# A gated attention and mixer kernel on one core: the order of the last four output parts, and of the first K chunk's pieces

## The chip, the core and the metric

The kernel runs on one core of a Trainium2 chip. The core has five engines that run side by side and meet at semaphores: TensorE (PE, with its weight loads shown apart as PEld), VectorE (DVE), ScalarE (ACT), GpSimd (POOL) and SyncE (SP), which only issues DMAs here. ACT issues a few DMAs as well. Products land in PSUM, which PE writes and DVE and ACT read; the rest lies in SBUF. The metric is the device time of one execution in microseconds, as the median of several runs.

## The reference, cut to what matters

Two blocks work on the same x (2048 rows, 640 columns), and a gate per row mixes their outputs.

```python
g = sigmoid((x * gate_w).sum(-1, keepdims=True))
# A: linear attention, 32 heads of 20
q, k, v = split(x @ wqkv)
pq, pk = phi(q), phi(k)               # phi(t) = (t+1 if t>0 else exp(t)) + 1e-6
num = pq @ (pk^T v);  den = pq . sum(pk) + 1e-6
a = (num / den) @ wo
# B: two layer norms, a shift of four column groups over the rows
x1 = x + shifted(gelu(layernorm(x) @ w1)) @ w2
b = x1 + gelu(layernorm(x1) @ w3) @ w4          # w3: 640 x 1728, w4: 1728 x 640
out = g * a + (1 - g) * b
```

The gate's sum over x * gate_w is itself a product with one column. The kernel hangs gate_w on to K's weights as column 640, so that the second half of each K product is 321 columns wide, not 320.

## The kernel before, in words

The 2048 rows are cut into 16 chunks of 128 rows (c) and into 4 tiles of 512 rows (t), so that a tile has four chunks (cc = 0 to 3). The 640 columns are five pieces of 128 (dc). All bf16 operands stay in SBUF. The schedule is written out by hand: each engine runs its instructions in the order in which the program issues them, and semaphores are put where tiles are shared. A read of a tile and a later write of the same tile are ordered by the tile as a whole, also where they touch different halves of it.

PSUM is handed out as four pairs of banks, by `pair()` (line 69): a tile of 128 x 2 x 512 floats, one bank for each half.

**The start.** SP loads chunk 0 of x as it is (line 126), two pieces of wk (dc 1 and 3), and then the transposed x, chunk by chunk and then in blocks of two and four chunks, by transposing DMAs (line 133); the block for chunks 8 to 11 is the sixth of the seven. ACT loads the gate vector as five rows of 128 (`g5`, line 127) and wk's pieces 0, 2 and 4. In the meantime PE runs products of a constant that nothing reads (`warmup`, lines 204 to 209): six of 512 columns and three of 128. Chunk 0 of x is turned by PE itself (line 215), in two groups of two and three pieces, each copied to SBUF by DVE (line 216). Between the groups PE turns the gate vector, with five rows as weights (line 218), and DVE copies it into column 640 of each piece of wk (line 219). After three more fillers of 128 columns, `k_mm` (line 190) runs chunk 0 piece by piece, dc = 0 to 4, two halves each, with a filler of 256 columns after each piece but the last (line 224). `k_evac` (line 197) applies phi on ACT and DVE. Chunks 1 to 15 follow without fillers (line 226), each with ten products; the first of a chunk waits for its transposed x.

**The middle** (Q, the attention's sums, the first layers of the mixer, and per tile w3, attention and w4) is not touched.

**The end.** `w4_tile(t)` (line 516) makes the last product of a tile: 13 products of 128 rows for each chunk and half, and a rest (`w4_rest`). It finishes chunks 0 and 2 first and then 1 and 3. For the last tile the odd chunks' halves are uneven: half 1 has 512 columns and half 0 has 128 (`w4_dst`, line 477). Each such part is finished on its own by `w4_part` (line 506): DVE scales it, adds the rest of the sum and writes it to `oc` (line 512), and SP stores it (line 514). The order of the four parts is given by line 531, as (chunk, half).

Of the kernel before, what the change touches and what calls it, by code (L numbers as in the profile page):

```python
# [9 lines left out]
BF16 = mybir.dt.bfloat16  # L10
# [6 lines left out]
def kernel(  # L17
# [13 lines left out]
    nc = tc.nc  # L31
    P = 128
    S, D = A_x.shape[1], A_x.shape[2]
# [6 lines left out]
    DC = D // P  # L40
    HD = D // 2
# [19 lines left out]
    const = ctx.enter_context(tc.tile_pool(name="const", bufs=1))  # L61
# [7 lines left out]
    def pair():  # L69
        return ps.tile([P, 2, 512], F32, name="pp")  # L70
# [13 lines left out]
    rb = const.tile([P, NT, TS], BF16)  # L84
    r_bf = const.tile([P, TS], BF16)
    ident = const.tile([P, P], BF16)
    g5 = const.tile([DC, P], BF16)
    mhalf = const.tile([P, CPT], F32)
    hmask = const.tile([P, H], F32)
    zbd = const.tile([P, DC, H], BF16)  # L90
# [16 lines left out]
    wk_sb = st1.tile([P, DC, D + 16], BF16)  # L107
# [7 lines left out]
    sp, aq, gq = nc.sync, nc.scalar, nc.gpsimd  # L115

    def load_x(c0, c1):
        sp.dma_start(x_sb[:, c0:c1, 0:D], x2[c0 * P:c1 * P, :].rearrange("(c p) d -> p c d", p=P))
# [4 lines left out]
    def load_wk(q, dc):  # L123
        q.dma_start(wk_sb[:, dc, 0:D], A_wqkv[dc * P:(dc + 1) * P, D:2 * D])

    load_x(0, 1)
    aq.dma_start(g5[:], gate_w.rearrange("(c p) -> c p", p=P))
    load_wk(sp, 1)
    load_wk(aq, 0)
    load_wk(aq, 2)  # L130
# [50 lines left out]
    def phi(dst, src, n):  # L181
        e = e_p.tile([P, 1024], BF16, name="e")
        ev = e[:, 0:n]
        if len(src.shape) == 3:
            ev = ev.rearrange("p (h e) -> p h e", h=src.shape[1])
        nc.scalar.activation(ev, src, ACT.Exp)  # L186
        nc.vector.tensor_scalar(e[:, 0:n], e[:, 0:n], 1.0, 1e-6, op0=ALU.min, op1=ALU.add)
        nc.vector.scalar_tensor_tensor(dst, src, 0.0, ev, op0=ALU.max, op1=ALU.add)  # L188

    def k_mm(pt, c, dcs, hfs=(0, 1), last=DC - 1):  # L190
        for dc in dcs:
            for hf in hfs:
                n = HD + hf
                nc.tensor.matmul(pt[:, hf, 0:n], lhsT=xT[:, dc, c * P:(c + 1) * P],  # L194
                                 rhs=wk_sb[:, dc, hf * HD:hf * HD + n], start=(dc == 0), stop=(dc == last))

    def k_evac(pt, c):
        nc.scalar.copy(ylog[:, c:c + 1], pt[:, 1, HD:HD + 1])
        phi(pk[:, c, :].rearrange("p (h e) -> p h e", h=2), pt[:, :, 0:HD], D)

    warm = pair()
    one = nc.const_aps.tensor(1.0, (P, TS), BF16)

    def warmup(n, w=TS):
        for i in range(n):
            nc.tensor.matmul(warm[:, 1, 0:w], lhsT=one[:, 0:P], rhs=one[:, 0:w], start=True, stop=True)  # L206

    warmup(6)
    warmup(3, P)
    kp = pair()  # L210
    turns = [(pair()[:, 0, :].bitcast(BF16), a, b) for a, b in ((0, 2), (2, DC))]
    tg = warm[:, 0, :].bitcast(BF16)
    for n, (ptb, a, b) in enumerate(turns):
        for dc in range(a, b):
            nc.tensor.transpose(ptb[:, (dc - a) * P:(dc - a + 1) * P], x_sb[:, 0, dc * P:(dc + 1) * P], ident[:])
        nc.vector.tensor_copy(xT[:, a:b, 0:P], ptb[:, 0:(b - a) * P].rearrange("p (c s) -> p c s", c=b - a))
        if n == 0:
            nc.tensor.transpose(tg[:, 0:DC], g5[:], ident[0:DC, 0:DC])
            nc.vector.tensor_copy(wk_sb[:, :, D], tg[:, 0:DC])
    warmup(3, P)  # L220
    for dc in range(DC):
        k_mm(kp, 0, (dc,))
        if dc < DC - 1:
            warmup(1, 2 * P)
    k_evac(kp, 0)
    for c in range(1, NCH):
        pt = pair()
        k_mm(pt, c, range(DC))
        k_evac(pt, c)
# [208 lines left out]
    def x1_scale(t, cc):  # L438
        c = t * CPT + cc
        x1 = st[t]["x1"][cc]  # L440
        nc.scalar.activation(x1[:], x1[:], ACT.Copy, scale=omg[:, c:c + 1])
# [27 lines left out]
    def w3_rest(t, dst):  # L469
        for dc in range(DC):  # L470
            for v in range(2):
                nc.tensor.matmul(dst[FR * v:FR * (v + 1), :], lhsT=w3_sb[:, dc, FF * P:F],  # L472
                                 rhs=st[t]["lnT"][:, dc, v * LT:(v + 1) * LT], start=(dc == 0), stop=(dc == DC - 1))
        st[t]["h2x"] = h2x_p.tile([P, LT], BF16, name="h2x")
        nc.scalar.activation(st[t]["h2x"][:], dst, ACT.Gelu_apprx_tanh)  # L475
# [5 lines left out]
    def w4_mm(t, cc, pts, hf, start):  # L481
        dst, a, b = w4_dst(t, cc, pts, hf)
        for fc in range(FF):
            nc.tensor.matmul(dst, lhsT=st[t]["h2"][:, fc * TS + cc * P:fc * TS + (cc + 1) * P],  # L484
                             rhs=w4_sb[:, fc, a:b], start=start and fc == 0, stop=not start and fc == FF - 1)

    def w4_rest(t, pts):
        for u in range(2):
            for hf in range(2):
                for v in range(2):  # L490
                    rows = slice(FR * v, FR * (v + 1))
                    dst, a, b = w4_dst(t, u + 2 * v, pts, hf)
                    nc.tensor.matmul(dst, lhsT=st[t]["h2x"][rows, u * P:(u + 1) * P],  # L493
                                     rhs=w4_sb[rows, FF, a:b], start=u == 1, stop=u == 0)

    def w4_out(t, cc, pt):
        c = t * CPT + cc
        x1 = st[t]["x1"][cc]
        oc = outp.tile([P, D], BF16, name="oc")
        nc.vector.scalar_tensor_tensor(oc[:], pt[:].rearrange("p h e -> p (h e)")[:, TS - LT:TS - LT + D],  # L500
                                       omg[:, c:c + 1], x1[:], op0=ALU.mult, op1=ALU.add)
        nc.sync.dma_start(out2[c * P:(c + 1) * P, :], oc[:])
# [3 lines left out]
    def w4_part(t, cc, pts, hf):  # L506
        c = t * CPT + cc
        src, a, b = w4_dst(t, cc, pts, hf)
        if cc not in ocs:
            ocs[cc] = outp.tile([P, D], BF16, name="oc")  # L510
        oc = ocs[cc]
        nc.vector.scalar_tensor_tensor(oc[:, a:b], src, omg[:, c:c + 1], st[t]["x1"][cc][:, a:b],  # L512
                                       op0=ALU.mult, op1=ALU.add)
        nc.sync.dma_start(out2[c * P:(c + 1) * P, a:b], oc[:, a:b])

    def w4_tile(t):
        pts = {cc: pair() for cc in (0, 2)}
        for cc in (0, 2):
            if t + 1 < NT:
                x1_scale(t + 1, cc)  # L520
            for hf in range(2):
                w4_mm(t, cc, pts, hf, True)
        for cc in (1, 3):
            pts[cc] = pair()
        w4_rest(t, pts)
        if t + 1 < NT:
            w3_rest(t + 1, pts[0][:, 0, 0:LT])
        for cc in (0, 2):
            w4_out(t, cc, pts[cc])
        last = t == NT - 1  # L530
        for cc, hf in ((3, 1), (1, 1), (1, 0), (3, 0)) if last else ((1, 0), (1, 1), (3, 0), (3, 1)):
            if t + 1 < NT and hf == 0:
                x1_scale(t + 1, cc)
            w4_mm(t, cc, pts, hf, False)
            if last:
                w4_part(t, cc, pts, hf)
            elif hf == 1:
                w4_out(t, cc, pts[cc])
# [22 lines left out]
    for t in range(NT):  # L561
        for i in range(NW3):
            w3_unit(t, i)
            if i < CPT and t + 1 < NT:
                w2_unit(t + 1, i)
            if 2 <= i < 2 + CPT:
                att_unit(t, i - 2)
        if t + 1 < NT:
            ln2_rstd(t + 1, 0, CPT)
            for cc in range(CPT):  # L570
                ln2_apply(t + 1, cc)
        if t == 0:
            w3_rest(0, pair()[:, 0, 0:LT])
        w4_tile(t)
# [30 lines left out]
```

## Time and profile before

| what | us |
|---|---|
| median of 4 runs (266.45 to 266.5) | 266.47 |
| the profiled execution's own time | 266.47 |
| its span, first to last instruction | 264.8 |
| PE busy in it | 260.3 |
| DVE busy | 139.5 |
| ACT busy | 85.1 |
| mean DMA flow over the span | 89 GB/s |

The span is what the profile's rows can explain; what lies around it (1.7 us here) belongs to the start and end of the execution. Times in the rows count from the first instruction. A matmul's length in a row contains the time until its result is written, so lengths of neighbours overlap: the distance between starts is what each costs PE. "Idle before" with an arrow names the last thing that an engine waited for. In the timeline several instructions of one line are merged into one row, with the idle time ahead of the first. The chain of waits is followed back from the last instruction, and it shows which engine set the time at each point.

### The profile page before, as it was taken

The numbers are of one execution on the slowest core, as the hardware profiler recorded it, in microseconds if no ns is written. First come the engines' busy times: TensorE is split into PE (matmuls) and PEld (weight loads), VectorE is DVE, ScalarE is ACT, GpSimd is POOL, SyncE is SP. The second block draws the span as 40 slices with busy tenths as digits, with TensorE's granted clock in tenths as the row PEclk, the third lists the DMA queues.
The fourth block names the chain that finished last, engine by engine and source line by source line (L and its number), as shares of the span: only waits on it lengthen the run. The fifth ranks groups of instructions, "written<-read, shape, count | busy, mean of one in ns | idle before, by whom it ended". The sixth has DMA issues, their size and how long they took to land.

```text
span 264.8 us, 4272 instructions
## 1 busy us (share of the span) xinstructions
PE 260.3 (98%) x1744; PEld 161.7 (61%) x1744; DVE 139.5 (53%) x271; ACT 85.1 (32%) x126; POOL 21.8 (8%) x67
## 2 busy tenths in 40 slices
PE   8999999999999999999999999999999999999994
PEld 4777555788754644555667556667565667455743
DVE  1688678899858597955403464403455323112132
ACT  1555544321165636622502222412131422233000
POOL 7100120012210140001000001000001000000000
PEclk9999999999999999999999999999999999999999
DMA  7999988045663526600132000042000041100011
GB/s 199 172 199 369 375 239 324 0 34 122 125 105 67 78 51 182 216 0 2 25 74 77 25 0 2 0 99 77 25 0 2 1 99 55 46 0 2 0 50 50
DMA packets 46285, 23.62 MB, mean 89 GB/s; under 512 B 35770, under 2 KB 45626, under 8 KB 46266
## 3 DMA queue, kind: packets, MB, share of 16 engines
q1 hardware_dynamic: 45824, 22.86, 34.2%
q10 hardware_dynamic: 442, 0.49, 0.5%
q8 instruction: 13, 0.21, 0.3%
q14 instruction: 6, 0.05, 0.1%
HBM read 12.21 MB, written 2.62 MB: 56 GB/s over the span
## 4 chain that ended last, share of the span: by engine, by line
PE 97%; ACT 1%; DVE 0%; issue 0%
PE pp L484 22%; PE pp L464 21%; PE pp L194 8%; PE pp L311 8%; PE pp L417 8%; PE pp L448 8%; PE pp L345 8%; PE pp L236 8%; PE pp L206 2%; PE pp L472 1%; PE pp L493 1%; ACT m_sb L385 1%; PE pp L364 1%; PE pp L251 0%; DVE oc L512 0%; PE pp L383 0%
## 5 line engine op out<-in xcount | busy, mean ns | idle before, releaser
L464 PE MATMUL pp<-lnxT,w_sb 128*128 128x512 bf16 x260 | 60.4, 379 | 0.0
L484 PE MATMUL pp<-w_sb,h 128*128 128x256 bf16 (+3 forms) x416 | 58.0, 299 | 0.8 <-DVE oc L512 0.8
L466 ACT ACTIVATE h<-pp 128x1024 bf16<-128x1024 f32 (+1 forms) x28 | 27.0, 963 | 82.2 <-PE pp L464 82.2
L484 PEld LDWEIGHTS <-h 128*128 128x128 bf16 x416 | 39.3, 98 | 18.8 <-issue 2.2
L464 PEld LDWEIGHTS <-w_sb 128*128 128x128 bf16 x260 | 25.5, 98 | 26.8
L500 DVE SCALAR_TENSOR_TENSOR oc<-pp,omg,x 128x640 bf16<-128x640 f32 x14 | 12.0, 881 | 41.4 <-ACT h2x L475 21.3
L451 DVE SCALAR_TENSOR_TENSOR x<-pp,gate,x 128x640 f32<-128x640 f32 x16 | 13.9, 867 | 29.4 <-PE pp L448 29.4
L420 DVE TENSOR_TENSOR x<-pp,x_sb 128x640 f32<-128x640 f32 x16 | 13.1, 820 | 22.6 <-PE pp L417 22.6
L186 ACT ACTIVATE e<-pp 128x640 bf16<-128x640 f32 (+1 forms) x26 | 21.5, 827 | 9.6 <-PE pp L236 9.6
L448 PE MATMUL pp<-m_sb,pqT 128*128 128x320 bf16 x160 | 24.3, 299 | 0.0
L417 PE MATMUL pp<-w_sb,hsT 128*128 128x320 bf16 x160 | 23.9, 299 | 0.1
L194 PE MATMUL pp<-wk_sb,xT 128*128 128x320 bf16 (+1 forms) x160 | 22.9, 303 | 0.0
L311 PE MATMUL pp<-x_sb,pk 128*128 128x320 bf16 (+1 forms) x160 | 22.3, 300 | 0.0
L236 PE MATMUL pp<-xT,hsT 128*128 128x512 bf16 x100 | 21.7, 379 | 0.0
L311 PEld LDWEIGHTS <-pk 128*128 128x128 bf16 x160 | 18.8, 117 | 3.5
L417 PEld LDWEIGHTS <-hsT 128*128 128x128 bf16 x160 | 15.7, 98 | 8.2 <-issue 0.2
L448 PEld LDWEIGHTS <-pqT 128*128 128x128 bf16 x160 | 15.7, 98 | 7.7
L194 PEld LDWEIGHTS <-xT 128*128 128x128 bf16 x160 | 15.7, 99 | 6.2 <-DMA xT<-in_A_x_dram 0.2
L345 PE MATMUL pp<-lnxT,w_sb 128*128 128x512 bf16 x80 | 17.9, 379 | 0.0
L236 PEld LDWEIGHTS <-hsT 128*128 128x128 bf16 x100 | 11.8, 118 | 9.7
L281 POOL TENSOR_SCALAR rstd<-mv 128x4 f32<-128x4 f32 (+1 forms) x11 | 3.5, 314 | 156.3 <-DVE mv L287 156.3
L188 DVE SCALAR_TENSOR_TENSOR pk<-pp,e 128x640 bf16<-128x640 f32 x16 | 13.2, 824 | 1.7
(77 smaller groups left out, 194.9 us busy)
## 6 DMA issues: line engine op xcount, KB each, us to landing
out_dram<-oc SPq DMA_DIRECT2D x14, 160.0 KB, 1.8
w_sb<-in_B_w_dram SPq DMA_DIRECT2D x1, 2080.0 KB, 10.2
w_sb<-in_B_w_dram SPq DMA_DIRECT2D x1, 1296.0 KB, 7.7
x_sb<-in_A_x_dram SPq DMA_DIRECT2D x2, 640.0 KB, 10.4
x_sb<-in_A_x_dram SPq DMA_DIRECT2D x1, 1120.0 KB, 8.0
wo_sb<-in_A_wo_dram SPq DMA_DIRECT2D x6, 160.0 KB, 7.2
w_sb<-in_B_w_dram SPq DMA_DIRECT2D x1, 864.0 KB, 5.0
hsT<-in_A_wqkv_dram SPq DMA_DIRECT2D x1, 800.0 KB, 5.5
```

The costliest lines, as they stand in the source:

```text
L186: nc.scalar.activation(ev, src, ACT.Exp)
L188: nc.vector.scalar_tensor_tensor(dst, src, 0.0, ev, op0=ALU.max, op1=ALU.add)
L194: nc.tensor.matmul(pt[:, hf, 0:n], lhsT=xT[:, dc, c * P:(c + 1) * P], rhs=wk_sb[:, dc, hf * HD:hf * HD + n], start=(dc == 0), stop=(dc == ...
L236: nc.tensor.matmul(pt[:, t % 2, :], lhsT=wq_sb[:, dc, :].rearrange("p (m j) -> p j m", j=DC)[:, j], rhs=xT[:, dc, t * TS:(t + 1) * TS], st ...
L311: nc.tensor.matmul(pt[:, hf, 0:HD + hf], lhsT=w, rhs=x_sb[:, c, hf * HD:(hf + 1) * HD + hf], start=(c == 0), stop=(c == NCH - 1))
L345: nc.tensor.matmul(pt[:, i, :], lhsT=w, rhs=lnxT[t][:, dc, :], start=(dc == 0), stop=(dc == DC - 1))
L417: nc.tensor.matmul(pt[:, hf, 0:HD], lhsT=hsT[:, fc, 2 + c * P:2 + (c + 1) * P], rhs=w2_sb[:, fc, hf * HD:(hf + 1) * HD], start=(fc == 0), ...
L448: nc.tensor.matmul(pt[:, hf, 0:HD], lhsT=pqT[:, j, c * P:(c + 1) * P], rhs=m_sb[:, j, hf * HD:(hf + 1) * HD], start=(j == 0), stop=(j == D ...
L451: nc.vector.scalar_tensor_tensor(x1, pt[:, :, 0:HD], gate[:, c:c + 1], x1, op0=ALU.mult, op1=ALU.add)
L464: nc.tensor.matmul(pt[:, k, :], lhsT=w3_sb[:, dc, fc * P:(fc + 1) * P], rhs=lnT[:, dc, :], start=(dc == 0), stop=(dc == DC - 1))
L466: nc.scalar.activation(h2[:, 2 * i * TS:(2 * i + n) * TS], pt[:].rearrange("p h e -> p (h e)")[:, 0:n * TS], ACT.Gelu_apprx_tanh)
L484: nc.tensor.matmul(dst, lhsT=st[t]["h2"][:, fc * TS + cc * P:fc * TS + (cc + 1) * P], rhs=w4_sb[:, fc, a:b], start=start and fc == 0, stop ...
```

## The change

It does three things. In the last tile, the four parts of the odd chunks run as (1,1), (3,1), (1,0), (3,0) in place of (3,1), (1,1), (1,0), (3,0). The gate vector lies in a full 128 x 128 tile, of which DVE clears all before ACT's DMA fills five rows, and PE turns it by a product with the identity's first five columns, into the second bank of the second group's PSUM tile, after that group's transposes; DVE copies it after that group's copy. And the fillers and the order of chunk 0's pieces differ: five fillers of 512 columns at first, four of 128 ahead of the K products, and the pieces in the order 1, 0, 3, 2, 4 with a filler of 128 columns ahead of the third, fourth and fifth.

```diff
-    g5 = const.tile([DC, P], BF16)
+    g5 = const.tile([P, P], BF16)
...
-    aq.dma_start(g5[:], gate_w.rearrange("(c p) -> c p", p=P))
+    nc.vector.memset(g5[:], 0.0)
+    aq.dma_start(g5[0:DC, :], gate_w.rearrange("(c p) -> c p", p=P))
...
-    def k_mm(pt, c, dcs, hfs=(0, 1), last=DC - 1):
+    def k_mm(pt, c, dcs, first=0, last=DC - 1):
         for dc in dcs:
-            for hf in hfs:
+            for hf in range(2):
                 n = HD + hf
                 nc.tensor.matmul(pt[:, hf, 0:n], lhsT=xT[:, dc, c * P:(c + 1) * P],
-                                 rhs=wk_sb[:, dc, hf * HD:hf * HD + n], start=(dc == 0), stop=(dc == last))
+                                 rhs=wk_sb[:, dc, hf * HD:hf * HD + n], start=(dc == first), stop=(dc == last))
...
+    k0_order = (1, 0, 3, 2, 4)
...
-    warmup(6)
+    warmup(5)
     warmup(3, P)
     kp = pair()
-    turns = [(pair()[:, 0, :].bitcast(BF16), a, b) for a, b in ((0, 2), (2, DC))]
-    tg = warm[:, 0, :].bitcast(BF16)
-    for n, (ptb, a, b) in enumerate(turns):
+    turns = [(pair(), a, b) for a, b in ((0, 2), (2, DC))]
+    for pt, a, b in turns:
+        ptb = pt[:, 0, :].bitcast(BF16)
         for dc in range(a, b):
             nc.tensor.transpose(ptb[:, (dc - a) * P:(dc - a + 1) * P], x_sb[:, 0, dc * P:(dc + 1) * P], ident[:])
+        if b == DC:
+            nc.tensor.matmul(pt[:, 1, 0:DC], lhsT=g5[:], rhs=ident[:, 0:DC], start=True, stop=True)
         nc.vector.tensor_copy(xT[:, a:b, 0:P], ptb[:, 0:(b - a) * P].rearrange("p (c s) -> p c s", c=b - a))
-        if n == 0:
-            nc.tensor.transpose(tg[:, 0:DC], g5[:], ident[0:DC, 0:DC])
-            nc.vector.tensor_copy(wk_sb[:, :, D], tg[:, 0:DC])
-    warmup(3, P)
-    for dc in range(DC):
-        k_mm(kp, 0, (dc,))
-        if dc < DC - 1:
-            warmup(1, 2 * P)
+        if b == DC:
+            nc.vector.tensor_copy(wk_sb[:, :, D], pt[:, 1, 0:DC])
+    warmup(4, P)
+    for n, dc in enumerate(k0_order):
+        if n > 1:
+            warmup(1, P)
+        k_mm(kp, 0, (dc,), first=k0_order[0], last=k0_order[-1])
     k_evac(kp, 0)
...
-        for cc, hf in ((3, 1), (1, 1), (1, 0), (3, 0)) if last else ((1, 0), (1, 1), (3, 0), (3, 1)):
+        for cc, hf in ((1, 1), (3, 1), (1, 0), (3, 0)) if last else ((1, 0), (1, 1), (3, 0), (3, 1)):
```

## The prediction

> **What bounds the kernel now.** The page first: its span, and TensorE's (PE's) share of it.
>
> ```profile
> span 264.8 us, 4272 instructions
> PE 260.3 (98%) x1744; PEld 161.7 (61%) x1744; DVE 139.5 (53%) x271; ACT 85.1 (32%) x126; POOL 21.8 (8%) x67
> ```
>
> PE is the chain nearly everywhere, so an edit pays only if it takes time from PE and if PE does not then wait for something else. The change touches two places: the first 7 us and the last 5. I read the end first, in the chain of waits (start, length, what).
>
> ```profile
> 253.89 5.73 PE pp L484 x26
> 259.62 0.02 issue
> 259.64 0.76 DVE oc L512
> 260.41 0.04 issue
> 260.45 1.63 PE pp L484 x26
> 262.07 0.02 issue
> 262.10 0.35 DVE oc L512
> ```
>
> For once DVE is in the chain: PE stands still between its 26 wide (512 columns) and its 26 narrow (128 columns) products. PE's timeline gives the stall and its releaser.
>
> ```profile
> 260.45 1.61 PE L484 MATMUL pp<-w_sb,h 128*128 128x128 bf16 x26 [0.84 <-DVE oc L512]
> ```
>
> The first narrow group (chunk 1, half 0) writes the same PSUM tile that DVE reads for chunk 1's half 1, which PE has just finished; the wait is for that read.
>
> Now the beginning, in the same chain.
>
> ```profile
> 0.83 3.04 PE pp L206 x9
> ...
> 4.08 0.12 PE pp L218
> ...
> 5.03 0.54 PE pp L194 x2
> 5.56 0.21 PE pp L206
> ...
> 6.24 0.27 PE pp L194 x2
> 6.51 0.11 PE pp L206
> ```
>
> Two K products take 0.54 us at 5.03 and 0.27 at 6.24; a 256-column filler 0.21 and then 0.11. PE runs at half pace until about 5.8, though the page's clock row shows full speed for the whole span: here the pace has to be read from the lengths. Only the chain's L194, L215 and L218 pieces are work; the rest is filler. Then I looked for the next place after that at which PE waits. It is in the timeline of PE's weight loads.
>
> ```profile
> 15.02 1.46 PEld L194 LDWEIGHTS <-xT 128*128 128x128 bf16 x11
> 16.66 1.34 PEld L194 LDWEIGHTS <-xT 128*128 128x128 bf16 x11 [0.18 <-DMA xT<-in_A_x_dram]
> ```
>
> At 16.66, K chunk 8 waits for its transposed x. That transpose is issued on SP at 9.73 and takes this long to land:
>
> ```profile
> xT<-in_A_x_dram SPq DMA_TRANSPOSE x1, 6.9
> ```
>
> 9.73 + 6.9 = 16.63, and the load follows at 16.66. So before the change PE arrives at chunk 8 almost exactly as its data does. In the DMA view of 13 to 17 us (slices of 0.1 us) one sees why it lands so late:
>
> ```profile
> GB/s 233 287 282 289 287 292 287 289 289 287 292 292 297 352 31 77 92 79 97 110 105 138 154 174 133 72 44 36 28 10 8 10 10 172 289 292 294 289 287 289
> q8 instruction: 1, 0.02, 1.8%
> ```
>
> From 14.4 to 16.3 the flow drops from about 290 GB/s to a quarter of that (the 19 slices sum to 1408 against 19 x 290 = 5510), and one fetch of instructions falls in this window. The drop costs 1.9 x (1 - 1408/5510) = 1.4 us; without it the tile would land near 15.2.
>
> **The change, part by part.**
>
> *End: odd chunks alternate.* The order of the last four groups becomes (1,1), (3,1), (1,0), (3,0). The same 52 products run, on the same tiles. Group (1,0) now needs only the read of (1,1), which in DVE's timeline runs from 256.84 for 0.75 us, long before. So (1,0) starts one product (0.216 us, as 5.6 us / 26) after the last wide product's start at 259.23: at 259.44, and its 13 products, 0.056 us apart (1.63 less the last one's 0.22 drain, over 25), end their starts at 260.17. Group (3,0) writes chunk 3's tile, whose read still ends at 260.40; it starts at 260.45, exactly when (1,0) started before. What is gone is one group's 13 x 0.056 = 0.73 us out of a stall of 0.84; the wait is not removed but covered by (1,0), except for 0.28 us. Bounds: 0 if (1,0) waited still, 0.73 + 0.28 = 1.01 if (3,0) did not wait. I take 0.73. Behind it: DVE's narrow part of chunk 1 (0.35) now follows the wide part of chunk 3 and ends near 260.75, while the last part cannot start before 261.37. On SP the four stores of 0.33 us each are issued behind their parts, at about 260.42, 260.80 and 261.75, with a gap of 0.6 before the last. Both covers would have to lose 0.6 us to cost anything. The last store is of the same size (32 KB, 1.4 us to landing in the DMA view), and the barrier behind it is unchanged. End: -0.73.
>
> *Beginning, on PE.* Removed: a 512 filler, 0.427 at half pace (weight loads of L206 start at 1.21, 1.64, 2.06). With it gone the fillers end at 3.24, and the transposes need x: issued 0.79, landing after 2.4, so 3.2. They start near 3.27 instead of 3.66. The gate vector's 5-row turn held the transposes up: the third one starts at 4.13, not at 3.77 + 0.107 = 3.88, and the next filler then waited for DVE's copy (4.55, not 4.42). The full product has the shape of its neighbours, so I price it as one (0.107; bounds 0.05 for five columns alone and the old 0.26). From the first transpose to the first K product: 5 + 1 + 4 fillers = 10 x 0.107 = 1.07, against 1.16. First K product: 4.34 against 4.82. Then two pieces at half pace (4 x 0.267), a filler, one more product to 5.8, and seven at 0.136 with two fillers of 0.055: chunk 0 ends near 6.57, and chunk 1 cannot begin before its own tile, 2.18 + 4.4 = 6.58. So 6.62 against 7.11: 0.49 us earlier.
>
> *Beginning, on ACT, DVE and SP.* The new memset on DVE has no row of its own; DVE's copies of 5 to 384 columns take 0.17 to 0.36 and POOL's memset of the identity 0.20. I take 0.2, bounds 0.1 and 0.36. Queued behind it on ACT are the gate's DMA (0.56), three loads of wk (1.32 together) and the table load (1.28), all later by it. Of the loads, the tightest is dc 4: 2.25 + 3.5 = 5.8, with the delay 6.0, needed at 6.3. The copy of the gate column, now last on DVE, ends near 4.6, when the second K product needs it at 4.61. If either is late, the price is its lateness, up to 0.2, and the 0.49 covers it. SP issues the same DMAs in the same order.
>
> *Where the 0.49 goes.* Chunks take 1.363 us each, so PE now reaches chunk 8 at 6.62 + 7 x 1.363 = 16.16, and its tile lands at 16.63 as before: SP's chain of transposes is untouched. The stall grows from 0.02 (matmul starts 0.153 apart where 0.136 is usual) to 0.5. From there on everything is as before. Net: -0.02. Bounds: +0.36 if the later ACT loads push the transposes' landing by as much as the memset's upper bound; -0.49 if the tile lands 0.5 earlier.
>
> [...]
>
> [...]
>
> *Sum.* -0.73 - 0.02 = -0.75 on the span of 264.76: 264.0. The profiled execution's own time is 266.47, 1.71 beyond its span; the median of the four runs shown is the same 266.47. Forecast: **265.7 us**.
>
> **The rivals.**
>
> *The beginning counts too* (12%): the drop in DMA flow is shorter or misses the tile, which lands by 16.1. For: no other K chunk waits for its tile. Against: the tile has been in flight since 13.1 at the latest (SP's issue of it ends there), so a drop that comes somewhat earlier meets it too. -0.73 - 0.51 = 265.2.
>
> *The tile lands later* (8%): the loads on ACT, shifted by 0.1 to 0.36, mix with the transposes. +0.1 to +0.36 on the forecast, 265.8 to 266.1; twice that, 266.4, if it happens to two tiles in a row. Against: the same bytes in the same queues.
>
> *The pace doubles later* (7%), the slower side. PE has run from 0.83 to about 5.8, 4.97 us, before it reaches full pace, and the change thins what runs there. If the 4.97 counted only from the first K product, at 4.34, the step would come at 9.3, 3.5 late; half pace over 3.5 us loses 1.75, of which 0.49 is covered: +1.26 - 0.73 = +0.53, 267.0. It decides once the step is over 2 x (0.49 + 0.73) = 2.4 us late. Against: PE's gaps before 5.8 shrink (the 0.25 and 0.13 at the gate's turn go, a wait of 0.03 for x comes).
>
> [...]
>
> *The end does not do what it says* (4%): (1,0) waits for the latest read all the same. 266.45.
>
> **How the numbers follow.** The forecast's case has 69%, its own range 265.5 to 266.0. A change under 0.2% (0.53 us) cannot be told from none: faster means below 265.94. That is most of the forecast's case and the first rival, 0.78; the late tile, the unmoved end and the forecast's upper edge make 0.13 the same; the late pace and what lies beyond make 0.09. The range 265.2 to 266.2 leaves out the late pace, the unmoved end and the far ends of the first two rivals.
>
> **What would show it.** In the profile after: no stall between the wide products and (1,0), and one of some 0.28 before (3,0); the last DVE part 4.53 after the first of the four (261.37 - 256.84), where it was 5.26; K chunk 1 at 6.6; PE's weight loads idle about 0.5 us for xT at chunk 8, at 16.6. I am wrong if that stall is missing, if K products still take 0.27 us after 6.5, or if a wait of 0.8 us remains at the end.

## The result and the profile after

The changed kernel took 267.19 us in the median (35 executions, 266.37 to 268.88), the kernel before 266.51 on the same occasion: a ratio of 1.0031, with a 95% interval of 1.0022 to 1.0040. By the ratio it is some 0.8 us slower (the two medians lie 0.7 us apart), where 0.75 us less was forecast. It also scatters: the kernel before stays within 266.15 and 267.1 but for one execution.

The profiled execution took 266.3 us and is among the fastest of the changed kernel, so its rows show the mechanism but not all of its price. From the page:

```profile
span 264.6 us, 4272 instructions
PE 259.9 (98%) x1743; PEld 161.6 (61%) x1743; DVE 139.6 (53%) x272; ACT 85.1 (32%) x126; POOL 21.8 (8%) x67
```

The end, in the chain of waits (start, length, what); lines 487 and 515 are the old 484 and 512:

```profile
254.41 5.73 PE pp L487 x26
260.14 0.03 issue
260.17 0.76 DVE oc L515
260.93 0.04 issue
260.98 0.90 PE pp L487 x13
261.88 0.02 issue
261.90 0.35 DVE oc L515
```

DVE is still in the chain, but behind it stand 13 narrow products, not 26. From the start of DVE's wide part to that of its last part it is 261.90 - 260.17 = 1.73 us, where it was 262.10 - 259.64 = 2.46: 0.73 us less. That is the end as predicted, to the hundredth.

The beginning, in the same chain:

```profile
0.88 0.12 DVE g L127
...
1.02 0.56 ACTq L128
...
1.61 0.39 ACTq L124
...
2.02 0.44 ACTq L124
...
2.50 4.86 DMA wk_sb<-in_A_wqkv_dram
...
7.40 6.70 PE pp L195 x48
```

Before, PE was in this chain from 0.83 on. Now the chain begins with the memset, goes through ACT's queue (ACTq, which issues the gate's DMA and the three loads of wk) and through the last of these loads, and PE enters at 7.40. PE's timeline shows what it did meanwhile (start, length, instructions, in brackets the idle time ahead and what ended it):

```profile
4.22 0.75 PE L195 MATMUL pp<-wk_sb,xT 128*128 128x320 bf16 x2
5.44 0.70 PE L195 MATMUL pp<-wk_sb,xT 128*128 128x320 bf16 x2 [0.47 <-DMA wk_sb<-in_A_wqkv_dram]
...
6.75 0.22 PE L208 MATMUL pp<-const-bfloat16-1.0 128*128 128x128 bf16 x1
7.40 1.79 PE L195 MATMUL pp<-wk_sb,xT 128*128 128x320 bf16 x12 [0.43 <-DMA wk_sb<-in_A_wqkv_dram]
```

The first K product comes at 4.22, earlier than forecast (4.34). Then PE stands still twice for a load of ACT's: for piece 0 before 5.44 and for piece 4 before 7.40. By the DMA view, this is how long ACT's last load took from issue to landing, first in the kernel before and then in the changed one:

```profile
wk_sb<-in_A_wqkv_dram ACTq DMA_DIRECT2D x1, 160.0 KB, 3.5
```

```profile
wk_sb<-in_A_wqkv_dram ACTq DMA_DIRECT2D x1, 160.0 KB, 4.9
```

It is issued at 2.50 where it was 2.25, and lands at 7.36 where it was 5.78: 0.25 us later in, 1.6 us later out. Chunk 1 starts at 7.67 (7.11 before), and the wait at chunk 8 is gone, as PE's weight loads show, which run through from 7.40 to 20.03:

```profile
7.40 12.63 PEld L195 LDWEIGHTS <-xT 128*128 128x128 bf16 x93 [0.55 <-issue]
```

Chunk 8's tile landed at 16.47, as before within 0.2 us. PE is simply later than it: chunk 8 starts at 17.20, not 16.67. The balance of the two profiles is +0.54 at chunk 8 and -0.73 at the end, -0.19 on the span (264.76 to 264.57). The median of the changed kernel lies 0.9 us above this execution, and that part had to be looked for in other runs.

### The profile page after: what moved, and what is told of

Read it like the earlier page. It is cut to its first block, busy times and chain, and to the rows that moved or that the text cites. A ratio compares the mean times of both kernels' runs of the same rounds, so it can differ in the third digit from the quotient of the medians.

```text
span 264.6 us, 4272 instructions
## 1 busy us (share of the span) xinstructions
PE 259.9 (98%) x1743; PEld 161.6 (61%) x1743; DVE 139.6 (53%) x272; ACT 85.1 (32%) x126; POOL 21.8 (8%) x67
## 4 chain that ended last, share of the span: by engine, by line
PE 95%; DMA 2%; ACT 1%; ACTq 1%; DVE 0%; issue 0%
PE pp L487 21%; PE pp L467 21%; PE pp L314 8%; PE pp L420 8%; PE pp L451 8%; PE pp L348 8%; PE pp L239 8%; PE pp L195 8%; DMA wk_sb<-in_A_wqkv_dram 2%; PE pp L475 1%; PE pp L496 1%; ACT m_sb L388 1%; PE pp L367 1%; PE pp L254 0%; DVE oc L515 0%; ACTq L124 0%
## 5 line engine op out<-in xcount | busy, mean ns | idle before, releaser
L314 PEld LDWEIGHTS <-pk 128*128 128x128 bf16 x160 | 18.8, 117 | 3.5
L451 PEld LDWEIGHTS <-pqT 128*128 128x128 bf16 x160 | 15.7, 98 | 7.7
L195 PEld LDWEIGHTS <-xT 128*128 128x128 bf16 x160 | 15.7, 99 | 7.5 <-issue 1.5
L348 PE MATMUL pp<-lnxT,w_sb 128*128 128x512 bf16 x80 | 17.9, 379 | 0.0
L188 DVE TENSOR_SCALAR e<-e 128x640 bf16<-128x640 bf16 (+1 forms) x26 | 9.5, 367 | 9.6 <-ACT e L187 8.0
```

The lines of the kernel that those rows point to most:

```text
L314: nc.tensor.matmul(pt[:, hf, 0:HD + hf], lhsT=w, rhs=x_sb[:, c, hf * HD:(hf + 1) * HD + hf], start=(c == 0), stop=(c == NCH - 1))
L348: nc.tensor.matmul(pt[:, i, :], lhsT=w, rhs=lnxT[t][:, dc, :], start=(dc == 0), stop=(dc == DC - 1))
L451: nc.tensor.matmul(pt[:, hf, 0:HD], lhsT=pqT[:, j, c * P:(c + 1) * P], rhs=m_sb[:, j, hf * HD:(hf + 1) * HD], start=(j == 0), stop=(j == D ...
```

## The experiments

Two theories stood against each other. *Wait*: the gate's DMA, first in ACT's queue, waits for the memset, ACT's loads come late, and PE stands still for them. *Fillers*: PE has too little work in the first microseconds, so that its clock is lifted late or lowered again. Each table row is the median, the ratio to the kernel before on the same chip with its interval (again not quite that of the medians), and how many executions had a mean granted clock of at most 0.995 (none of the kernel before had, beside any of e1 to e16). A clock that is merely lifted late does not show in that column: the records begin with the lift, and the profiled executions of e3, e7 and e9, where it came only at 9.89, 9.27 and 9.51 us, have a mean clock of 0.999.

| run | us | ratio | clock 0.995 or less |
|---|---|---|---|
| changed kernel | 267.19 | 1.0031 (1.0022 to 1.0040) | 7 of 36 |
| e1 new end alone | 265.72 | 0.9970 (0.9959 to 0.9980) | 0 of 7 |
| e2 new start alone | 267.50 | 1.0049 (1.0028 to 1.0071) | 2 of 10 |
| e3 gate last | 268.55 | 1.0063 (1.0041 to 1.0084) | 2 of 6 |
| e4 wait alone | 266.81 | 1.0014 (1.0001 to 1.0028) | 0 of 12 |
| e5 no wait | 265.89 | 0.9967 (0.9954 to 0.9980) | 0 of 6 |
| e6 gate second | 266.14 | 0.9984 (0.9971 to 0.9997) | 0 of 11 |
| e7 a load ahead | 266.35 | 0.9986 (0.9974 to 0.9999) | 0 of 12 |
| e8 changed, again | 267.85 | 1.0050 (1.0029 to 1.0070) | 5 of 12 |
| e9 longer wait | 268.69 | 1.0080 (1.0054 to 1.0107) | 4 of 6 |
| e10 tile split | 265.61 | 0.9952 (0.9940 to 0.9965) | 0 of 6 |
| e11 parts 176 | 265.57 | 0.9953 (0.9939 to 0.9968) | 0 of 6 |
| e12 both | 265.64 | 0.9954 (0.9940 to 0.9968) | 0 of 6 |
| e13 loads on SP | 267.08 | 1.0004 (0.9983 to 1.0025) | 0 of 10 |
| e14 transpose early | 268.11 | 1.0027 (1.0000 to 1.0053) | 5 of 10 |
| e15 long fillers | 266.98 | 1.0005 (0.9996 to 1.0013) | 0 of 12 |
| e16 changed, third | 267.06 | 1.0017 (1.0002 to 1.0031) | 1 of 11 |

**e1 and e2: the two halves.** e1 is the kernel before with the new order of the last four parts; e2 is the changed kernel with the old order.

```diff
-        for cc, hf in ((3, 1), (1, 1), (1, 0), (3, 0)) if last else ((1, 0), (1, 1), (3, 0), (3, 1)):
+        for cc, hf in ((1, 1), (3, 1), (1, 0), (3, 0)) if last else ((1, 0), (1, 1), (3, 0), (3, 1)):
```

> The kernel before with the new order of the last four parts alone. Both theories of the slow start (the wait for the memset ahead of ACT's loads; the shorter fillers) leave this one out of it: 0.73 us less than before, so 265.75, and no more scatter than before. If the time is not below 266.2, the end is not worth what the sum of the prediction said.

> The changed kernel with the old order of the last four parts: all of the new start, nothing of the new end. If the two add up, 267.19 + 0.73 = 267.9, with the scatter of the changed kernel (2.5 us between fastest and slowest).

The end alone gives 265.72, a ratio of 0.9970: 0.8 us, 0.5 to 1.1 by the interval, which holds the 0.73. The start alone costs 1.0049, 1.3 us (0.7 to 1.9). All of the loss is in the start.

**e4: the wait alone.** The kernel of e1 plus the 128-row tile, its memset and the wait; the old fillers, order and five-row turn.

```diff
-    g5 = const.tile([DC, P], BF16)
+    g5 = const.tile([P, P], BF16)
...
+    nc.vector.memset(g5[:], 0.0)
+    aq.dma_start(g5[0:DC, :], gate_w.rearrange("(c p) -> c p", p=P))
```

> The kernel before with the new end, and of the new start only the 128-row tile, its memset and the wait of the gate's DMA for it; fillers, order of the pieces and the five-row turn are the old ones. Theory 'wait': ACT's loads land 0.5 to 1.6 us late and chunk 1 starts near 7.7 although PE has its long fillers: 266.2 to 267.2. Theory 'fillers': as the kernel with the new end alone, 265.75.

1.0014 against e1's 0.9970: the memset and its wait alone cost 1.2 us. *Wait* said that, and *fillers* said 265.75. ACT's last load landed at 7.87, and PE waits for it in spite of all the old fillers:

```profile
7.91 1.39 PE L195 MATMUL pp<-wk_sb,xT 128*128 128x320 bf16 x9 [0.59 <-DMA wk_sb<-in_A_wqkv_dram]
```

Chunk 1 starts at 8.18, later than the 7.7 that *wait* named.

**e5: the changed kernel without the wait.**

```diff
-    g5 = const.tile([P, P], BF16)
+    g5 = const.tile([DC, P], BF16)
...
-    nc.vector.memset(g5[:], 0.0)
-    aq.dma_start(g5[0:DC, :], gate_w.rearrange("(c p) -> c p", p=P))
+    aq.dma_start(g5[:], gate_w.rearrange("(c p) -> c p", p=P))
...
-            nc.tensor.matmul(pt[:, 1, 0:DC], lhsT=g5[:], rhs=ident[:, 0:DC], start=True, stop=True)
+            nc.tensor.matmul(pt[:, 1, 0:DC], lhsT=g5[:], rhs=ident[0:DC, 0:DC], start=True, stop=True)
```

> The changed kernel without memset and wait: the gate's tile has five rows again and the product in its new place contracts over these five; fillers, order of the pieces and the end are the changed kernel's. Theory 'wait': ACT's loads land as in the kernel before (the last by 5.8 to 6.5 us), chunk 1 starts by 7.1, the time is 265.5 to 265.8 and no execution has a mean clock of 0.994. Theory 'fillers': still 266.7 to 267.2, and some executions at 268.5.

265.89, no execution with a lower clock, ACT's last load landed at 6.21: the short fillers and the new order do no harm when nothing waits. They bring nothing either, for e5 (0.9967) is e1 (0.9970). Its profile shows why, in PE's weight loads:

```profile
13.91 2.28 PEld L194 LDWEIGHTS <-xT 128*128 128x128 bf16 x17
16.79 3.25 PEld L194 LDWEIGHTS <-xT 128*128 128x128 bf16 x25 [0.60 <-DMA xT<-in_A_x_dram]
```

Chunk 1 starts at 6.81, 0.3 us earlier than before, and at chunk 8 PE's weight loads wait 0.6 us for the transposed tile (0.43 us of PE's own time). This is the wait that the prediction foresaw for the changed kernel; it appears as soon as the other one is taken away.

**e3 and e6: the gate's DMA later in ACT's queue,** so that the memset is done when its turn comes. In e6 it stands behind the first load, as the diff shows, in e3 behind all three.

```diff
     nc.vector.memset(g5[:], 0.0)
-    aq.dma_start(g5[0:DC, :], gate_w.rearrange("(c p) -> c p", p=P))
     load_wk(sp, 1)
     load_wk(aq, 0)
+    aq.dma_start(g5[0:DC, :], gate_w.rearrange("(c p) -> c p", p=P))
```

> The changed kernel, with the gate's DMA behind ACT's three loads of wk instead of ahead of them; the memset stays. Theory 'wait': the loads are issued from 0.8 us again and land as before (the last near 5.8), chunk 0 no longer stalls, chunk 1 starts near 6.6, chunk 8 waits for its transposed x until 16.6, and the time is 265.75 with little scatter. Theory 'fillers' (too little work on PE in the first 6 us, the clock is lifted late or lowered again): still about 267.2, with mean clocks of 0.994 in some executions.

> The changed kernel with ACT's first load of wk ahead of the gate's DMA, which then finds the memset done, so that nothing in ACT's queue stands still. Theory 'wait': loads issued at 0.8, 1.8 and 2.25 land by 3.9, 5.4 and 6; the gate, issued 0.2 us later than in the changed kernel, lands near 4 and may hold PE for some tenths: 265.7 to 266.1. Theory 'fillers': 267.2 as before, with executions at a mean clock of 0.994.

e3 missed by far, and for a reason that the edit brought in itself. ACT's loads did land as in the kernel before (the last at 5.73), but the gate landed near 6, and everything in PE's order stood behind its product. From PE's timeline of e3:

```profile
3.78 0.71 PE L217 MATMUL pp<-ident,x_sb 128*128 128x128 bf16 x5 [0.34 <-DMA x_sb<-in_A_x_dram]
6.00 0.17 PE L219 MATMUL pp<-ident,g 128*128 128x5 bf16 x1 [1.51 <-DMA g<-in_gate_w_dram]
```

Its time says nothing on the wait; the landing does. e6, with the gate between, came to 266.14, close to what *wait* said. In both, x itself landed at 3.7, not near 3.1, with ACT's first load running beside it; whether that is the cause no run shows.

**e9: a longer wait.** The memset covers 128 x 1024 in place of 128 x 128, and ACT's first DMA is issued at 1.49, not 1.02.

```diff
-    g5 = const.tile([P, P], BF16)
+    g5w = const.tile([P, 8 * P], BF16)
...
-    nc.vector.memset(g5[:], 0.0)
+    nc.vector.memset(g5w[:], 0.0)
```

> The changed kernel with a memset eight times as large ahead of the gate's DMA (128 x 1024 in place of 128 x 128): ACT's queue stands still some 0.45 us longer. If it is the lateness of ACT's loads that costs, PE stands still for them 0.5 us or more longer in chunk 0, with more executions at a mean clock of 0.994: 268 to 269. If the loss is a step that any wait brings about (an order on the queues that flips once), the time stays at that of the changed kernel, 267.2 to 267.9.

268.69, a ratio of 1.0080, and four of six executions with a lowered clock. The cost grew with the wait (e8, with the changed kernel's own wait, has 1.0050); it is not a step that any wait brings about. Not all of it is the loads' own lateness: in the profile of e9 the last one landed at 8.22, hardly later than in e8 (8.14), but the clock was lifted only at 9.51.

**e8: the changed kernel again, and the clock.**

> The changed kernel once more, beside the others on the same chip: 267.2 by both theories, with a fifth of the executions at 268.5 to 268.9 and a mean clock of 0.994.

Five of 12 executions had a mean clock of 0.994, and the profiled one (268.7 us, span 267.0) was one of them. Its windows (stretch in us; PE's busy time with the number of its instructions; granted clock; DMA share; GB/s), cut where the trace's clock records change:

```profile
0.00:4.67 4.67, 3.84 (x20) 1.00 0.57 142
4.67:8.08 3.41, 1.42 (x11) 1.00 1.24 187
8.08:11.49 3.41, 3.30 (x13) 0.50 1.04 214
11.49:15.00 3.51, 3.51 (x28) 1.00 1.15 187
```

The first record is at 4.67, where the clock is lifted; the 1.00 ahead of it stands for no record (PE's pace there is half: the five turns of x take 0.108 us each from 3.23 to 3.77, a filler of the same 128 columns 0.05 from 5.96 to 6.01). In the next 3.41 us PE is busy for only 1.42, since it waits 0.80 and 1.30 us for two of ACT's loads, and then the clock is taken back for another 3.41 us, in which PE does 13 products at half pace (3.30 / 13 = 0.25 us each). Chunk 8 starts at 19.60, 2.93 us later than before; with -0.73 at the end, that is the +2.2 us of this span. From chunk 1 to chunk 8 it takes 10.92 us where the kernel before takes 9.55: 1.4 us are the clock's, the rest the stalls'.

PE was not idle in the stretch after which the clock was lowered: it was busy for 42% of it here (1.42 of 3.41 us), and for 42% in the profile of e14 (1.42 of 3.42 us), where the clock was lost too. In e16's profile, shown below, it was busy for 45% of the 3.41 us after the lift and kept the clock. Whether the busy share decides this, and where a limit would lie, no run here shows.

**e15 and e16: what the short fillers add.** e15 is the changed kernel with the old fillers, e16 the changed kernel beside it.

```diff
-    warmup(5)
+    warmup(6)
...
-        if n > 1:
-            warmup(1, P)
+        if n > 0:
+            warmup(1, 2 * P)
```

> The changed kernel, wait included, with the fillers of the kernel before: six of 512 columns at first and one of 256 after each of chunk 0's first four pieces. With the wait alone and all else old, no execution of 12 had a mean clock of 0.994; of the changed kernel 12 of 48 had. If the short fillers are what lets the clock be lowered while PE waits for ACT's loads, none or next to none is seen here, nothing at 268.5, and the median is 266.6 to 267.1, 0.5 to 1 below the changed kernel. If fillers are too short beside stalls of 0.5 to 1.3 us to matter, a quarter of the executions is at 0.994 here too and the median is the changed kernel's.

> The changed kernel beside it on the same chip: 267.2 to 267.9 and a quarter of the executions at a mean clock of 0.994, by both.

The medians hardly differ (266.98 and 267.06; intervals of the ratios 0.9996 to 1.0013 and 1.0002 to 1.0031), so the expected 0.5 to 1 us on the median did not come. With the wait and long fillers no execution of 24 (e4 and e15) had its clock lowered, and with the wait and short ones 15 of 69 did (the changed kernel, e2, e8, e16). At one rate of 15 in 69 for all, none in 24 has a chance of 0.3%. But the rate differs between occasions: 7 of 36, 2 of 10, 5 of 12, 1 of 11. On the two occasions that saw both kinds of filler (e4 beside e2, e15 beside e16) it is 0 of 24 against 3 of 21, which chance alone gives in 9% of cases. So *fillers* probably had a point, on top of *wait*: they do not set the median, but they may decide whether a late load also costs the clock. The profiles point the same way. This is the stretch of 3.41 us after the lift, first in e16 and then in e15:

```profile
4.97:8.38 3.41, 1.53 (x13) 1.00 1.27 201
```

```profile
5.50:8.91 3.41, 2.20 (x16) 1.00 1.20 183
```

PE is busy for 45% of it with short fillers and for 64% with long ones; both kept the clock.

**e7, e13 and e14: why 0.25 us becomes 1.6.** In e7 SP issues the last load ahead of its transposing DMAs, in e13 all five (the order of the pieces stays); in e14, which is e5 otherwise, SP's first transposing DMA stands one place earlier, ahead of its second load. The first hunk is e7, the second e14.

```diff
-    load_wk(aq, 4)
+    load_wk(sp, 4)
...
+    load_xT(1, 2)
     load_wk(sp, 3)
     load_wk(aq, 4)
-    for c0, c1 in ((1, 2), (2, 3), (3, 4), (4, 6), (6, 8), (8, 12), (12, 16)):
+    for c0, c1 in ((2, 3), (3, 4), (4, 6), (6, 8), (8, 12), (12, 16)):
```

> The changed kernel with memset and wait, but its last load of wk (dc 4) issued by SP ahead of the transposing DMAs, not by ACT behind the first of them. If a load is slow because it runs beside the transposing DMAs, it lands near 5.5 now, not at 7.4, chunk 1 starts near 7, and what is lost is the 0.45 us by which SP's transposes start later: chunk 8's tile at 17.0, time 266.0 to 266.3. If a load is late just by its own late issue, it lands 0.3 earlier than in the changed kernel and the time stays at 266.9 or more.

> The changed kernel, memset and wait included, with all five loads of wk on SP ahead of the transposing DMAs; on ACT only the gate's DMA waits. The landing of the last load is what is looked at. If loads are slow because they run beside the transposing DMAs, all five land by about 5.5 us, PE stalls for none of them, and what is lost instead is SP's transposes starting 1.2 us later (chunk 8's tile near 17.8): 266.6 to 267, no mean clock of 0.994. If any load is slow between 3 and 7 us, whatever runs beside it, the last lands at 7 or later and chunk 0 stalls as in the changed kernel.

> The kernel without the wait, with SP's first transposing DMA one place earlier (ahead of its load of dc 3), so that ACT's loads, issued as early as in the kernel before, meet it. If running beside the transposing DMAs is what makes loads slow, ACT's last load lands at 6.8 to 8 us and not at 5.8 to 6.5, and the time rises to 266.3 or more though nothing waits on ACT. If the lateness of ACT's own issue is what counts, ACT's loads land as before, and only SP's load of dc 3, issued some 1.3 us later, is late.

In e7 the last load landed at 6.91 (8.14 in e8 on the same chip, 7.36 in the changed kernel's first profile), and the time fell to 266.35, near what was said for loads out of the transposes' way. But the load landed much later than the 5.5 that was said, and it took 4.7 us from its issue, little less than the 4.9 to 5.6 us of the kernels with the wait; part of the gain is just its earlier issue (2.17, not 2.50). The profiled execution of e7 is also one of its slowest (267.31), with the clock lifted only at 9.27. In e13 the last landed at 6.67, between the two expectations, in 3.5 us from its issue; the clock held (none of 10 at 0.995 or less), and PE's waits for the late transposes, 0.30 us before 7.44 and 0.25 before 11.96, took back some of what had been saved. In e14 ACT's last load took 4.6 us and landed at 6.86, against 4.0 and 6.21 in e5 (3.5 to 4.2 us in the kernel before, e1, e5, e10, e11 and e12, which issue it at the same time), at the low end of what was expected, and 268.11 is due above all to SP's own load, as PE's timeline of e14 shows:

```profile
5.03 0.22 PE L208 MATMUL pp<-const-bfloat16-1.0 128*128 128x128 bf16 x1
7.19 0.43 PE L195 MATMUL pp<-wk_sb,xT 128*128 128x320 bf16 x2 [1.94 <-DMA wk_sb<-in_A_wqkv_dram]
```

The packet records do not settle it. A 1280-byte packet on ACT's queue takes 55 to 56 ns in the kernel before, by half-microsecond means. In the changed kernel it takes 79 to 116 ns from 5.0 to 6.5, when transposing packets (256 bytes) run beside it. But such packets run from 4.5 or 5.0 on in the kernel before, e1, e5 and e7 too, and from 5.0 to 5.5 ACT's packets beside them take 55 ns there. So their company alone does not make a load slow. There is a second thing in the flow from 2 to 8 us (slices of 0.15 us), the kernel before first:

```profile
GB/s 68 234 367 384 239 145 111 256 393 393 367 333 273 307 401 393 401 367 367 369 352 297 268 193 258 260 203 285 137 224 76 68 162 280 273 207 52 0 15 85
```

```profile
GB/s 68 222 401 359 316 350 316 154 154 68 51 154 256 307 316 326 331 323 348 340 290 280 222 161 97 196 396 152 142 219 277 258 246 224 118 259 294 288 287 253
```

From 3.05 to 3.8 the changed kernel's flow drops to 51 to 154 GB/s, before any transposing packet; the kernel before has a shorter drop near 2.8. Most other profiles fit in time: with the wait on ACT ahead of its loads (e2, e4, e7, e8, e15, e16) the drop lies near 3.2 to 3.6, without it (e1, e5, e10, e11, e12, e14) near 2.6 to 3.0. So why the delay grows stays open: e7, e13 and e14 agree in sign with the transposes, none in full size, and the drop has no known cause. That the load itself takes longer with the wait is in every one of these profiles: ACT's last load takes 3.5 to 4.2 us in the kernel before, e1, e5, e10, e11 and e12, and 4.9 to 5.6 in the changed kernel, e2, e4, e8, e15 and e16.

**e10, e11 and e12: what is left in e5.** e10 cuts the transposed load of chunks 8 to 11 in two, e11 cuts the odd chunks' last parts at 176 columns, e12 does both.

```diff
-    for c0, c1 in ((1, 2), (2, 3), (3, 4), (4, 6), (6, 8), (8, 12), (12, 16)):
+    for c0, c1 in ((1, 2), (2, 3), (3, 4), (4, 6), (6, 8), (8, 10), (10, 12), (12, 16)):
...
-        n = D - TS if t == NT - 1 and cc % 2 else LT
+        n = 176 if t == NT - 1 and cc % 2 else LT
```

> The kernel without the wait (five-row gate tile, new fillers, new end) with the transposed load of chunks 8 to 11 cut into 8 and 9, and 10 and 11. If chunk 8's wait for its tile (0.43 us of PE in that kernel's profile, tile landed at 16.75) is what keeps the shorter start from counting, the first half lands by 16.2 or so, that wait goes, and the time is 265.4 to 265.6. If the drop in DMA flow near 14 to 16 us holds the half tile up just as long, it stays at 265.9.

> The kernel without the wait, with the odd chunks' halves of the last tile cut 176 to 464, not 128 to 512. The new end leaves a wait of some 0.28 us before the last group, since 13 narrow products (0.73) are shorter than DVE's read of the wide part (0.75 and its latency of 0.25). Wider narrow products (13 x 0.076 = 0.98) cover it: 0.2 us less, 265.7, after 0.05 to 0.1 more for the last part on DVE. If the wait has another cause, no change or 0.1 more.

> The last two together. If both act where they are thought to act, in different places, they add up: 265.2 to 265.4, and 0.5% below the kernel before.

In e10 the half tile landed at 14.55 and no wait is left at chunk 8 (16.46 in place of 16.79). In e11 the last wait for DVE is gone from the chain; PE runs all 52 products in one piece:

```profile
254.14 7.18 PE pp L486 x52
261.33 0.02 issue
261.35 0.40 DVE oc L514
```

Both places were the ones named. Their times, 265.61 and 265.57, lie 0.3 us below e5, but the intervals of all four overlap, and e12 (265.64) is not below either, so the sum that was expected of the two did not show. What can be said is that e10, e11 and e12 are 0.5% faster than the kernel before (0.9952 to 0.9954, upper ends 0.9965 to 0.9968).

## Why the prediction was wrong, by its own steps

*The end* (-0.73): right in mechanism and size, by the chain (2.46 to 1.73) and by e1 (0.8, 0.5 to 1.1). The remaining wait before group (3,0) is there too, and e11 removed it in the way that the step's own arithmetic suggests.

*The beginning, on PE*: nearly right. 6.62 was forecast for chunk 1; the same start without the wait has 6.81 in e5 and 6.54 to 6.86 in e10 to e12. One count in it is off: behind the product that ends at 5.8 the order 1, 0, 3, 2, 4 leaves five products, not the seven that are written, and only with five does the sum come to the 6.57 given.

*Where the 0.49 goes*: right, and hidden at first. Chunk 8's tile does not come earlier with an earlier PE (16.75 in e5, 16.88 in e11), and in e5 the earlier start vanishes in a wait of 0.6 us. The changed kernel does not show it because PE arrives 0.5 us late instead. The reason suggested for the late tile, an instruction fetch in the drop of the flow, does not hold: the drop comes without it (last section).

*The beginning, on ACT* is the step that failed: "If either is late, the price is its lateness, up to 0.2, and the 0.49 covers it." The lateness of the issue was sized well: 0.23 to 0.25 us, inside the 0.1 to 0.36. The error was to carry it to the landing one for one, with the old 3.5 us from issue to landing ("2.25 + 3.5 = 5.8, with the delay 6.0"). That duration belonged to the old times of issue, and it was the shortest of the six profiles that keep them (3.5 to 4.2). In the changed kernel the same load took 4.9 us, 5.6 in e8, and the lateness at landing was 1.6 to 2.4 us: more than three times the cover of 0.49. By e2 the whole start, put at -0.02, cost 1.3 us.

*The pace doubles later*, the rival on the slower side at 7%: near the truth in kind, wrong in its cause. It took the thinner warm-up as the danger. In e8 and e14 the clock was lowered after some 3.4 us in which PE, waiting for loads, was busy for 42%; with the same short fillers and nothing to wait for, e5 lost it in none of six. In e3, e7 and e9 the step itself came late, at 9.27 to 9.89, where the rival had put it at 9.3; there too PE had waited before it, for the gate in e3 (1.51 us) and for ACT's loads in e7 (0.78 us) and e9 (the last landed at 8.22). The 4.97 us before full pace, read from one profile, are no fixed figure: the trace's clock records have the step anywhere from 3.57 to 9.89 us in the profiles of this study, and from 3.57 to 6.09 in the kernels whose loads are not held up (e1, e5, e6, e10, e12 and the kernel before).

*The tile lands later* (8%) named ACT's shifted loads and the transposes, but let the transposes suffer, not the loads.

*The range*, 265.2 to 266.2, took the memset's bounds from DVE's rows alone. The bound that was missing is that of the last load's duration: 3.5 us before, 4.9 to 5.6 with the wait.

## What to carry to other kernels

In the changed kernel a wait ahead of the first instruction in ACT's DMA queue delayed that issue and the three behind it by 0.23 to 0.25 us, and the last load's time from issue to landing did not stay what it was: price such a time with a wide range. Neither its own old row (3.5 us) nor the slowest like load beside it (3.7) came near the 4.9 to 5.6 us that it took. Where PE waits for loads in its first microseconds, look at the executions' mean clocks as well as at the median, since in e8 3.41 us with PE busy for 42% were followed by 3.41 us at a granted clock of 0.50, and at the pace of the products, since lifts at 9.27 to 9.89 us (e3, e7, e9) left the mean at 0.999. And when a saving ends in a later wait, as at chunk 8 here (in e5 0.3 us earlier at chunk 1, then 0.43 us of waiting), it is worth nothing, however well it is made.

## What the runs showed of the hardware that was not expected

The clock was lifted at 3.57, 3.64, 3.69, 3.85, ... and as late as 9.89 us in the profiles of this study, and was lowered again for 3.41 us in two of them (e8, e14), each time after PE had stood still for 1.9 us or more since it was lifted. The mean granted clock of an execution tells of it: 0.994 of 267 us is 3.2 us at half pace.

One fetch of instructions at 14.4 us comes with a drop of the DMA flow for 1.9 us in the kernel before. It is not needed for the drop: in e3, e8, e9, e13 and e14 the fetch comes only at 17.3 to 18.8, and the flow drops between 14 and 17 all the same. This is e14's flow from 13 to 17 us (slices of 0.1 us), with its fetch at 17.4:

```profile
GB/s 287 287 289 294 289 292 287 287 289 292 292 289 134 72 120 108 105 120 56 92 189 172 120 108 97 110 212 261 289 289 282 276 289 287 292 292 287 289 287 292
```

The tile in flight lands at 16.4 to 16.9 in half of the profiles where it was loaded in one piece (15.7 to 17.9 in the others). What causes the drop is open.
